# Seven half-size products for the first layers of the last two experts, in an attention and mixture-of-experts kernel

## The chip, the cores and the metric

One NeuronCore of a Trainium2 chip runs the whole program. The metric is the device time of one execution in microseconds. The kernel before took 952.56 us (median of 3 runs, 950.79 to 954.71).

## What is computed

Attention over 8 batches and 12 heads (448 tokens each, head size 64) gives x, 3584 tokens of 768 numbers. A router assigns every token to one of 8 experts, at most 448 tokens each, greedily from the highest logit down. Each expert is two matrix products with a ReLU between them:

```python
for e in range(E):
    mask = assigned == e
    h = np.maximum(x[mask] @ w1[e], 0.0)     # 448 x 768 @ 768 x 1024
    out[mask] = h @ w2[e]                     # 448 x 1024 @ 1024 x 768
```

## The kernel before, in words

The first half of the time is attention. Then the experts are processed one by one (here counted 0 to 7 in that order; the router picks the next one while earlier ones are computed, and that work is over within expert 5's first layer).

Everything is f32 in effect but runs as f16 pairs: a value is a high half h and a residue l, and a product is three matmuls, h by h, l by h and h by l. The **first layer** (`hidden`, L1640) makes the 1024 rows of the hidden layer in 8 blocks f of 128: 6 pieces of 128 of the inner size x 3 matmuls, each 128 x 128 weights against 448 tokens, summed in one PSUM bank (`ph`, 3 banks in turn). ScalarE applies the ReLU and writes the f16 half `hh` (L1659), VectorE the residue `hl` (L1661). The **second layer** (`result`, L1672) has the tokens in three chunks of 128 and one of 64. A chunk is two halves of 384 columns, each 24 matmuls into a `py` bank (3 in turn); ScalarE copies each half to `y` (3 buffers), and GpSimd scatters the rows of `y` to the output. The 64-token chunk uses half the array for each half of the columns.

Weights of the next expert come while this one is computed. `fetch` (L1564) has SP issue a DMA of 768 KB of f32 into one of 4 `stage` buffers; `split` (L1581) has ScalarE write the f16 half (L1590) and VectorE the residue in two instructions of 768 elements (L1594). There are 8 such pieces per expert, 4 of w1 and 4 of w2. `gather` (L1600) has GpSimd collect the expert's tokens into `rows`; DMA transposes (L1610) turn them into `xt`, 6 pieces of high halves and 6 of residues.

What order the instructions have is settled as the program is written out: every matmul advances a clock of estimated time (`tick`, L1710), pieces that are due by it are placed (`feed`, L1765, gives the due times), and what follows on VectorE is placed when ScalarE should be done (`later`, L1741). Each engine then runs its own queue strictly in that order. `run` (L1798) goes through the experts.

Of the kernel before, what the change touches and what calls it, by code (L numbers as in the profile page):

```python
# [37 lines left out]
class Plan:  # L38
# [51 lines left out]
class Attention:  # L90
# [1446 lines left out]
class Experts:  # L1537
# [19 lines left out]
    def load(self, k):  # L1557
        T = self.T
        e = self.router.e[k]
        T["reg", k] = self.nc.sync.value_load(e[:1, :1], min_val=0, max_val=7)  # L1560
        for n, a, f in (("w1h", 6, 1024), ("w1l", 6, 1024), ("w2h", 8, 768), ("w2l", 8, 768)):
            T[n, k] = self.w.tile([128, a, f], F16, name=n)

    def fetch(self, k, i, later=False):  # L1564

        T = self.T
        r = T["reg", k]
        s = self.w.tile([128, 1536], F32, name="stage", bufs=self.STAGES)
        if later:
            self.nc.gpsimd.memset(s[:, 0:1], 0.0)  # L1570
        if i < 4:
            src = self.w1[bass.ds(r, 1), :, 256 * i:256 * i + 256].rearrange("o (c p) f -> p (o c) f", p=128)
            v = s.rearrange("p (c f) -> p c f", c=6)
        else:
            j = 2 * (i - 4)
            src = self.w2[bass.ds(r, 1), 128 * j:128 * j + 256, :].rearrange("o (c p) f -> p (o c) f", p=128)
            v = s.rearrange("p (c f) -> p c f", c=2)
        self.nc.sync.dma_start(v, src)
        T["stage", k, i] = v

    def split(self, k, i):  # L1581
        T = self.T
        v = T.pop(("stage", k, i))
# [12 lines left out]
        if i + self.STAGES < 8:  # L1596
            self.later(0.0, lambda: self.fetch(k, i + self.STAGES), k, i)


    def gather(self, k):  # L1600
        nc, T = self.nc, self.T
        idx = self.router.idx[k]
        T["xt", k] = self.w.tile([128, 12, 448], F16, name="xt")
# [194 lines left out]
    def run(self):  # L1798
# [28 lines left out]
        for k in range(8):  # L1827
            self.now = k
            self.start()
            for f in range(8):  # L1830
# [3 lines left out]
                self.hidden(k, f)  # L1834
            self.need(k, 7)
# [50 lines left out]
```

## Time and profile before

| | |
|---|---|
| time of the runs, median | 952.56 us |
| profiled execution, its own time | 953.22 us |
| its span, first to last instruction | 951.0 us |
| mean granted TensorE clock | 0.988 |
| TensorE (matmuls) busy | 892.6 us, 94% |
| VectorE busy | 700.3 us, 74% |
| ScalarE busy | 512.1 us, 54% |
| GpSimd busy | 468.9 us, 49% |

The profile is that of one execution, taken by the hardware profiler, so durations in it are set against 953.22 us. A share of busy time is an average over very different stages; the rows further down are cut by stage.

### The profile page before, as it was taken

The page shows a single profiled execution, that of the slowest core. Times are in us where ns is not written, and L with a number is a line of the kernel's source. Part 1 is how long each engine was busy: PE and PEld are TensorE (multiplying, and loading weights), DVE is VectorE, ACT ScalarE, POOL GpSimd, SP SyncE. Part 2 cuts the span into 40 slices and gives each one's busy share as a digit, 9 for nine tenths or more (in the row PEclk, how much of TensorE's full clock was granted, in tenths as well). Part 3 has the DMA queues.
Part 4 walks back from the last instruction along what each step waited for, and adds up shares of the span by engine and source line. Part 5 has one row for each costly group of instructions (what it writes and reads, how often), then busy time and mean ns, then how long its engine had stood idle before and what let it go on. Part 6 is the DMA issues. An engine that isn't in the chain of part 4 may idle for free.

```text
span 951.0 us, 24928 instructions
## 1 busy us (share of the span) xinstructions
PE 892.6 (94%) x10335; PEld 573.7 (60%) x10336; DVE 700.3 (74%) x1562; ACT 512.1 (54%) x942; POOL 468.9 (49%) x463
## 2 busy tenths in 40 slices
PE   2799999999999999998699999999999999999996
PEld 1367767676777767757355556555565555655553
DVE  6999998899989988888787787786776758234110
ACT  5998978897888788653042424333332424243111
POOL 6889998999999899994000302121112020120001
PEclk9999999999999999999699999999999999999999
DMA  7558999997999987771272919494947649593001
GB/s 193 118 122 161 180 162 221 189 210 129 240 203 194 158 198 165 134 146 64 77 249 73 325 41 298 123 291 147 259 156 222 202 155 282 167 182 114 26 17 42
DMA packets 264230, 157.74 MB, mean 166 GB/s; under 512 B 189876, under 2 KB 251316, under 8 KB 263092
## 3 DMA queue, kind: packets, MB, share of 16 engines
q1 hardware_dynamic: 258674, 133.66, 60.5%
q0 software_dynamic: 4608, 22.02, 6.8%
q8 instruction: 81, 1.33, 0.6%
q10 hardware_dynamic: 834, 0.46, 0.2%
q14 instruction: 33, 0.27, 0.1%
HBM read 94.42 MB, written 22.02 MB: 122 GB/s over the span
## 4 chain that ended last, share of the span: by engine, by line
issue 36%; PE 35%; DVE 12%; DMA 6%; POOL 6%; ACT 3%; SPq 1%; POOLq 0%; DVEq 0%; ACTq 0%
PE po L571 8%; PE psc L528 6%; PE ph L1669 6%; DVE mx L506 4%; DMA kq<-s 3%; PE pm L497 3%; POOL rows L1607 3%; PE py L1686 2%; POOL out_dram L1702 2%; PE po L577 2%; PE psc L530 2%; PE po L581 2%; PE po L579 2%; DVE vs L468 2%; ACT e L536 1%
## 5 line engine op out<-in xcount | busy, mean ns | idle before, releaser
L1669 PE MATMUL ph<-xt,w1h 128*128 128x448 f16 (+2 forms) x804 | 209.7, 344 | 0.8 <-ACT xt L1626 0.5
L506 DVE TENSOR_REDUCE mx<-pm 128x2 f32<-128x896 f32 x162 | 175.8, 1085 | 25.3 <-PE pm L497 24.3
L552 POOL TENSOR_TENSOR pl<-e 128x896 f16<-128x896 f32 x105 | 182.3, 1748 | 10.6 <-ACT e L536 9.4
L1702 POOL DMA_INDIRECT out_dram<-y,idx x32 | 33.2, 1036 | 311.4 <-ACT y L1688 239.0
L536 ACT ACTIVATE e<-psc 128x896 f32<-128x896 f32 x168 | 148.8, 911 | 48.9 <-PE psc L530 47.5
L571 PE MATMUL po<-v,e 128*128 128x65 f32 (+1 forms) x960 | 156.9, 279 | 0.0
L571 PEld LDWEIGHTS po<-v,e 128*128 128x128 f32 (+1 forms) x960 | 120.0, 176 | 33.2 <-issue 31.7
L1669 PE MATMUL ph<-xt,w1l 128*128 128x448 f16 (+2 forms) x402 | 136.8, 344 | 0.0
L579 PE MATMUL po<-vs,e 128*128 128x64 f16 (+1 forms) x1056 | 131.2, 194 | 0.1
L577 PE MATMUL po<-vs,e 128*128 128x65 f16 (+1 forms) x1056 | 130.8, 195 | 0.3 <-DVE z L603 0.3
L581 PE MATMUL po<-vs,pl 128*128 128x65 f16 (+1 forms) x1056 | 129.8, 193 | 0.0
L528 PE MATMUL psc<-kq 64*128 64x448 f16 (+1 forms) x1152 | 124.2, 352 | 2.1 <-ACT e L536 1.2
L1686 PE MATMUL py<-w2h,hh 128*128 128x384 f16 x384 | 125.0, 326 | 0.0
L1686 PE MATMUL py<-w2h,hl 128*128 128x384 f16 x384 | 125.0, 326 | 0.0
L1686 PE MATMUL py<-w2l,hh 128*128 128x384 f16 x384 | 125.0, 326 | 0.0
L1659 ACT ACTIVATE hh<-ph 128x448 f16<-128x448 f32 x64 | 34.8, 543 | 145.6 <-PE ph L1669 131.3
L577 PEld LDWEIGHTS <-e 128*128 128x128 bf16 (+1 forms) x1056 | 109.8, 120 | 2.9 <-issue 1.9
L1669 PEld LDWEIGHTS <-w1h 128*128 128x128 f16 x804 | 74.0, 97 | 61.3 <-issue 1.5
L1686 PEld LDWEIGHTS <-hh 128*128 128x128 f16 x768 | 73.6, 97 | 45.8
L1688 ACT ACTIVATE y<-py 128x384 f32<-128x384 f32 x48 | 23.5, 491 | 132.4 <-PE py L1686 104.9
L1661 DVE SCALAR_TENSOR_TENSOR hl<-ph,hh 128x448 f16<-128x448 f32 x64 | 39.2, 618 | 71.2 <-ACT hh L1659 71.2
L581 PEld LDWEIGHTS <-pl 128*128 128x128 f16 (+1 forms) x1056 | 90.1, 101 | 0.2 <-issue 0.2
(274 smaller groups left out, 1811.3 us busy)
## 6 DMA issues: line engine op xcount, KB each, us to landing
stage<-in_moe_w_dram SPq DMA_DIRECT2D x64, 768.0 KB
vraw<-in_v_dram SPq DMA_DIRECT2D x24, 384.0 KB
xd<-xa SPq DMA_DIRECT2D x8, 1152.0 KB
qkraw<-in_q_dram SPq DMA_DIRECT2D x11, 768.0 KB
qkraw<-in_k_dram SPq DMA_DIRECT2D x11, 768.0 KB
vraw<-in_v_dram SPq DMA_DIRECT2D x48, 32.0 KB
xd<-xa SPq DMA_DIRECT2D x16, 96.0 KB
qkraw<-in_q_dram SPq DMA_DIRECT2D x22, 64.0 KB
```

Of the source, the lines that this page charges most:

```text
L506: self.nc.vector.tensor_reduce(m, p[r, :, :448], axis=AX.X, op=OP.max)
L528: mm(o, k[r, mine], q[r, all_], start=i == 0, stop=False)
L536: self.nc.scalar.activation(e, p[:, :, :448], AF.Exp, scale=scale)
L552: eng.tensor_tensor(l, self.T["e", d], self.T["ph", d], op=OP.subtract)
L571: nc.tensor.matmul(out, self.T["e", d][:, h, q0:q0 + m], self.v32[g % 2][:, 2 * h + a, wide.index(b % 4)], start=first, stop=last)
L577: nc.tensor.matmul(out, e[:, h, q0:q0 + m], vh, start=first, stop=False)
L579: nc.tensor.matmul(out[:, :64], e[:, h, q0:q0 + m], vl[:, :64], start=False, stop=False)
L581: nc.tensor.matmul(out, l[:, h, q0:q0 + m], vh, start=False, stop=last)
L1661: self.later(0.6, lambda: nc.vector.scalar_tensor_tensor(hl, whole, 0.0, hh, op0=OP.max, op1=OP.subtract), k, 3.5, f)
L1669: nc.tensor.matmul(p, a, b[:, o], start=st, stop=sp)
L1686: nc.tensor.matmul(p, a[:, f, s], b[:, f, o], start=st, stop=sp)
L1702: st = nc.gpsimd.indirect_dma_start(out=self.out, out_offset=bass.IndirectOffsetOnAxis(ap=self.router.idx[k][:n, c:c + 1], axis=0), in_=y[ ...
```

## The change

For experts 6 and 7 alone, the first layer is computed with w1 cut in halves both ways (A11, A12, A21, A22, each 384 of the inner size by 512 hidden rows) and the tokens likewise (two halves of the inner size, two of 224 tokens). Seven products of halves replace eight: A11 B11, A12 B21, and five products of sums. In each of 4 blocks i of 128 hidden rows (in both halves of the hidden layer) a product is 9 matmuls of 224 columns into a PSUM bank of its own (3 `ph`, 2 `py`, 2 `rp`), and VectorE and ScalarE combine the seven in f32 partial sums that lie in `orow`, the router's tile of one-hot rows ("or" in the rows), used here as two times 3 x 224 f32. Each of these has one buffer for all blocks.

- `fetch` brings quarters of w1. Of these A11, A12 and A22 are split as they are; then VectorE forms the four sums of quarters in place in `stage` (4 operations of 128 x 1536 f32, L1630), and the four sums are split too (`quarter`).
- `tokens` forms the four sums of the token halves on VectorE and splits them again.
- The splits of the sums and of w2 (for expert 6) are placed in the second layer of the expert before; for expert 7, w2 is split during its own first layer.
- Weights all come from two tiles, "wh" and "wl", with 4 buffers each; `xt` has 3 buffers, `y` has 2 where it had 3.

```diff
+    def quarter(self, k, i):
+        if i == 3:
+            a11, a12, a22, a21 = (T["stage", k, j] for j in range(4))
+            for o, x, y, op in ((a22, a21, a22, OP.add), (a21, a11, a21, OP.subtract), (a11, a22, a11, OP.subtract),
+                                (a12, a12, a11, OP.subtract)):
+                self.later(1.65, lambda o=o, x=x, y=y, op=op: V.tensor_tensor(o, x, y, op=op), k, i)
+            return
...
+        nc.scalar.activation(h, v, AF.Copy, scale=self.WS)
+        self.scalar(1.48)
+        for w in (slice(0, 768), slice(768, 1536)):
+            self.later(0.93, lambda w=w: V.scalar_tensor_tensor(l[:, w], v[:, w], self.WS, h[:, w], op0=OP.mult,
+                                                                op1=OP.subtract), k, i)
+        if more:
+            self.later(0.0, lambda: self.fetch(k, 4 + n), k, i)
+
+    def tokens(self, k):
...
+        V.tensor_tensor(f, x[:, :6], x[:, 6:], op=OP.add)
+        for o, a, b in ((b11, b12, b11), (b12, b22, b12), (b22, b22, b11), (b21, b21, b22)):
+            V.tensor_tensor(o, a, b, op=OP.subtract)
+        for j in (0, 3):
+            nc.scalar.activation(y[:, j:j + 3], f[:, j:j + 3], AF.Copy)
+            V.tensor_tensor(y[:, 6 + j:9 + j], f[:, j:j + 3], y[:, j:j + 3], op=OP.subtract)
...
+    SUMMED = 5.0, 2.4
+    SECOND = 18.0, 4.0
...
+    def seventh(self, k, i, n, j, h, p):
...
+        for c in range(3):
+            for a, b, st, sp in ((w, 0, c == 0, False), (w, 6, False, False), (v, 0, False, c == 2)):
+                nc.tensor.matmul(p, a[:, c], x[:, b + 3 * j + c], start=st, stop=sp)
+                self.tick(0.095)
+
+    def hidden7(self, k, i):
...
+        p1, p2, p6, p5, p7, p3, p4 = (
+            self.ps.tile([128, 512], F32, name=n, bufs=2 if n == "rp" else 3)[:, :224]
+            for n in ("ph", "py", "rp", "ph", "py", "rp", "ph"))
+        t = self.router.orow.rearrange("p g a t -> p (g a t)").bitcast(F32)
+        c1, c2 = (t[:, 672 * n:672 * n + 672].rearrange("p (n t) -> p n t", n=3) for n in range(2))
...
+        def relu(f, v):
+            v = v.rearrange("p n t -> p (n t)")
+            A.activation(hh[:, f], v, AF.Relu)
+            self.scalar(0.55)
+            V.scalar_tensor_tensor(hl[:, f], v, 0.0, hh[:, f], op0=OP.max, op1=OP.subtract)
+
+        self.seventh(k, i, 0, 0, 0, p1)
+        m = c2[:, 0]
+        A.activation(m, p1, AF.Copy)
+        self.scalar(0.35)
+        self.seventh(k, i, 1, 1, 0, p2)
+        self.seventh(k, i, 3, 1, 1, p6)
+        add(c1[:, 0], m, p2)
+        add(c1[:, 2], m, p6)
+        self.seventh(k, i, 5, 0, 0, p5)
+        add(c1[:, 1], c1[:, 2], p5)
+        self.seventh(k, i, 6, 0, 1, p7)
+        add(c2[:, 2], c1[:, 2], p7)
+        add(c2[:, 1], c2[:, 2], p5)
+        self.seventh(k, i, 4, 1, 1, p3)
+        add(c1[:, 1], c1[:, 1], p3)
+        relu(i, c1[:, 0:2])
+        self.seventh(k, i, 2, 1, 0, p4)
+        add(c2[:, 0], c2[:, 2], p4)
+        relu(i + 4, c2[:, 0:2])
...
-        y = self.w.tile([128, 768], F32, name="y", bufs=3)
+        y = self.w.tile([128, 768], F32, name="y", bufs=2)
```

**The order on VectorE, late in expert 5's first layer.** "or" are the router's one-hot rows, "hl" a block's residue, "wl"/"w1l" a split of weights, "stage" the sums of weights. Before:

```order
L1491 TENSOR_TENSOR or<-ar,rows_9263 128x1536
L1594 SCALAR_TENSOR_TENSOR w1l<-stage,w1h 128x3x256 x2
L1661 SCALAR_TENSOR_TENSOR hl<-ph,hh 128x448 x2
L1594 SCALAR_TENSOR_TENSOR w1l<-stage,w1h 128x3x256
L1502 COPY idlo<-rp 128x4
L1504 SCALAR_TENSOR_TENSOR idx<-rp,idlo 128x4
```

With the change:

```order
L1491 TENSOR_TENSOR or<-ar,rows_9263 128x1536
L1797 SCALAR_TENSOR_TENSOR hl<-ph,hh 128x448
L1641 SCALAR_TENSOR_TENSOR wl<-stage,wh 128x768 x2
L1630 TENSOR_TENSOR stage<-stage 128x1536 x4
L1797 SCALAR_TENSOR_TENSOR hl<-ph,hh 128x448 x2
L1502 COPY idlo<-rp 128x4
L1504 SCALAR_TENSOR_TENSOR idx<-rp,idlo 128x4
```

The first "hl" is that of block 3 in both. The residue of block 4, next to it before, stands behind two splits and the four sums of expert 6's weights now. Ahead of this piece four splits have been placed since the residue of block 0, where there were two.

**The order on VectorE in expert 6's first layer,** from the last operations of block 1 to the third addition after the sums in block 2. Before (any part of that stage):

```order
L1594 SCALAR_TENSOR_TENSOR w1l<-stage,w1h 128x3x256 x2
L1661 SCALAR_TENSOR_TENSOR hl<-ph,hh 128x448
L1594 SCALAR_TENSOR_TENSOR w1l<-stage,w1h 128x3x256 x2
L1661 SCALAR_TENSOR_TENSOR hl<-ph,hh 128x448
L1594 SCALAR_TENSOR_TENSOR w1l<-stage,w1h 128x3x256 x2
```

With the change:

```order
L1713 SCALAR_TENSOR_TENSOR hl<-or,hh 128x448
L1641 SCALAR_TENSOR_TENSOR wl<-stage,wh 128x768 x2
L1707 TENSOR_TENSOR or<-or,ph 128x224
L1713 SCALAR_TENSOR_TENSOR hl<-or,hh 128x448
L1641 SCALAR_TENSOR_TENSOR wl<-stage,wh 128x768 x2
L1707 TENSOR_TENSOR or<-or,py 128x224
L1707 TENSOR_TENSOR or<-or,rp 128x224
L1630 TENSOR_TENSOR stage<-stage 128x1536 x4
L1707 TENSOR_TENSOR or<-or,ph 128x224
L1707 TENSOR_TENSOR or<-or,py 128x224
L1707 TENSOR_TENSOR or<-or,ph 128x224
```

Splits of expert 7's quarters and the four sums for expert 7 stand between the additions that read and so free the banks.

**The order on ScalarE in the same stage,** blocks 0 to 2 ("or" is the copy of p1, "hh" the ReLU, "wh" a split). Before:

```order
L1659 ACTIVATE hh<-ph 128x448 x2
L1590 ACTIVATE w1h<-stage 128x6x256
L1659 ACTIVATE hh<-ph 128x448
L1590 ACTIVATE w1h<-stage 128x6x256
L1659 ACTIVATE hh<-ph 128x448
```

With the change:

```order
L1717 ACTIVATE or<-ph 128x224
L1711 ACTIVATE hh<-or 128x448 x2
L1717 ACTIVATE or<-ph 128x224
L1638 ACTIVATE wh<-stage 128x1536 x2
L1711 ACTIVATE hh<-or 128x448 x2
L1638 ACTIVATE wh<-stage 128x1536
L1717 ACTIVATE or<-ph 128x224
L1711 ACTIVATE hh<-or 128x448 x2
```

Two splits stand between the copy and the ReLU of block 1, and a third ahead of the copy of block 2.

## Rows read from the trace of the kernel before

**Rows 1.** Busy time by stage: layers 1 and 2 of experts 5, 6, 7 (us).

```profile
core 0: us, PE busy (x) PEld busy (x) DVE busy (x) ACT busy (x) POOL busy (x), PEclk, DMA share, GB/s
776.20:805.50 29.30, 29.30 (x208) 16.15 (x207) 24.95 (x67) 11.64 (x14) 5.43 (x6) 1.00 1.05 285
805.50:833.00 27.50, 27.50 (x193) 16.62 (x191) 6.11 (x7) 7.60 (x10) 3.23 (x6) 1.00 0.55 188
833.00:860.30 27.30, 27.30 (x147) 14.13 (x146) 12.95 (x17) 11.64 (x14) 4.79 (x6) 1.00 0.94 204
...
887.80:915.00 27.20, 27.20 (x146) 14.09 (x145) 4.37 (x7) 4.77 (x9) 0.99 (x2) 1.00 0.04 8
```

**Rows 2.** Timeline of TensorE, matmuls of 128 and 448 columns: start, length.

```profile
482.98 0.28 PE L1669 MATMUL ph<-xt,w1h 128*128 128x128 f16 x2
...
483.14 0.28 PE L1669 MATMUL ph<-xt,w1h 128*128 128x128 f16 x2
...
888.75 0.35 PE L1669 MATMUL ph<-xt,w1l 128*128 128x448 f16 x1
...
889.32 0.35 PE L1669 MATMUL ph<-xt,w1l 128*128 128x448 f16 x1
```

**Rows 3.** Groups by shape since 440 us: count, busy us, mean ns, idle before.

```profile
L1669 PEld LDWEIGHTS <-w1h 128*128 128x128 f16 x804 | 74.0, 97 | 61.3 <-issue 1.5
...
L1594 DVE SCALAR_TENSOR_TENSOR w1l<-stage,w1h 128x768 f16<-128x768 f32 x64 | 59.3, 950 | 3.4 <-ACT w1h L1590 3.4
L1590 ACT ACTIVATE w1h<-stage 128x1536 f16<-128x1536 f32 x32 | 47.3, 1477 | 23.5 <-DVE placed L1453 21.0 <-DMA stage<-in_moe_w_dram 2.5
...
L1491 DVE TENSOR_TENSOR or<-ar,rows 128x1536 bf16<-128x1536 bf16 x8 | 7.6, 950 | 0.0
...
L1165 DVE SCALAR_TENSOR_TENSOR logits<-esel,logits 128x224 f32<-128x224 f32 x7 | 2.7, 383 | 0.0
...
L1245 DVE TENSOR_TENSOR or<-key,unit 128x640 f32<-128x640 f32 x2 | 1.6, 812 | 0.0
...
L1245 DVE TENSOR_TENSOR or<-key,unit 128x256 f32<-128x256 f32 x2 | 0.8, 407 | 0.0
```

**Rows 4.** Timeline of VectorE, expert 5's first layer.

```profile
792.77 2.08 DVE L1491 TENSOR_TENSOR or<-ar,rows 128x2048 bf16<-128x2048 bf16 x2
794.77 1.82 DVE L1594 SCALAR_TENSOR_TENSOR w1l<-stage,w1h 128x768 f16<-128x768 f32 x2
```

**Rows 5.** Timeline of ScalarE: ReLU of expert 5's block 6, two results of expert 7.

```profile
802.30 0.54 ACT L1659 ACTIVATE hh<-ph 128x448 f16<-128x448 f32 x1 [2.42 <-PE ph L1669]
...
919.19 0.49 ACT L1688 ACTIVATE y<-py 128x384 f32<-128x384 f32 x1 [3.41 <-PE py L1686]
...
926.99 0.49 ACT L1688 ACTIVATE y<-py 128x384 f32<-128x384 f32 x1 [3.46 <-PE py L1686]
```

**Rows 6.** Timeline of all engines, end of expert 7's first layer.

```profile
914.85 0.35 PE L1669 MATMUL ph<-xt,w1l 128*128 128x448 f16 x1
...
915.24 0.54 ACT L1659 ACTIVATE hh<-ph 128x448 f16<-128x448 f32 x1 [2.86 <-PE ph L1669]
...
915.82 0.62 DVE L1661 SCALAR_TENSOR_TENSOR hl<-ph,hh 128x448 f16<-128x448 f32 x1 [2.78 <-ACT hh L1659]
```

**Rows 7.** DMA issues of the page, weights.

```profile
stage<-in_moe_w_dram SPq DMA_DIRECT2D x64, 768.0 KB
```

**Rows 8.** Timeline of GpSimd, first scatter of expert 7.

```profile
923.81 0.97 POOL L1702 DMA_INDIRECT out_dram<-y,idx  x1 [33.61 <-ACT y L1688]
```

**Rows 9.** Busy time by microsecond near the end, columns as in rows 1.

```profile
927.00:928.00 1.00, 1.00 (x8) 0.59 (x7) 0.00 (x0) 0.48 (x1) 0.00 (x0) 1.00 0.00 0
...
942.00:943.00 1.00, 0.63 (x8) 0.20 (x4) 0.00 (x0) 0.28 (x1) 0.00 (x0) 1.00 0.05 18
...
948.00:949.00 1.00, 0.00 (x0) 0.00 (x0) 0.00 (x0) 0.00 (x0) 0.00 (x0) 0.50 0.00 0
```

More of the change, by code (lines that the diff above doesn't have):

```diff
@@ L1570, in fetch @@
             self.nc.gpsimd.memset(s[:, 0:1], 0.0)
-        if i < 4:
+        if k in self.SEVEN and i < 4:
+            a, b = self.QUARTERS[i]
+            src = self.w1[bass.ds(r, 1), 384 * b:384 * b + 384, 512 * a:512 * a + 512]
+            src = src.rearrange("o (c p) f -> p (o c) f", p=128)
+            v = s.rearrange("p (c f) -> p c f", c=3)
+        elif i < 4:
             src = self.w1[bass.ds(r, 1), :, 256 * i:256 * i + 256].rearrange("o (c p) f -> p (o c) f", p=128)
@@ L1582, in split @@
         T = self.T
+        if k in self.SEVEN and i < 4:
+            return self.quarter(k, i)
         v = T.pop(("stage", k, i))
@@ L1597, in split @@
             self.later(0.0, lambda: self.fetch(k, i + self.STAGES), k, i)
+    SEVEN = 6, 7
+    QUARTERS = (0, 0), (0, 1), (1, 1), (1, 0)
+    SUMS = {3.2: 0, 3.4: 1, 3.6: 2, 3.8: 3}
+    def quarter(self, k, i):
+        nc, T = self.nc, self.T
+        V = nc.vector
+        if i == 3:
[4 more added lines that the diff above has]
+            return
+        if i == 3.05:
+            return self.tokens(k)
+        more = i > 3
+        n = self.SUMS[i] if more else i
+        v = T["stage", k, n].rearrange("p c f -> p (c f)")
+        h, l = (T[w, k + 0.5 * more].rearrange("p a f -> p (a f)")[:, 1536 * n:1536 * n + 1536] for w in ("w1h", "w1l"))
+        nc.scalar.activation(h, v, AF.Copy, scale=self.WS)
[5 more added lines that the diff above has]
+            self.later(0.0, lambda: self.fetch(k, 4 + n), k, i)
@@ new lines, in tokens @@
+    def tokens(self, k):
+        nc, T = self.nc, self.T
+        V = nc.vector
+        x, y = T["xt", k], T["xt", k + 0.5]
+        f = self.w.tile([128, 4, 1536], F16, name="rows", bufs=1).rearrange("p c d -> p (c d)").bitcast(F32)
+        f = f[:, :2688].rearrange("p (n c) -> p n c", n=6)
+        b11, b12, b21, b22 = (f[:, 3 * j:3 * j + 3, 224 * h:224 * h + 224] for j in (0, 1) for h in (0, 1))
+        V.tensor_tensor(f, x[:, :6], x[:, 6:], op=OP.add)
[4 more added lines that the diff above has]
+            V.tensor_tensor(y[:, 6 + j:9 + j], f[:, j:j + 3], y[:, j:j + 3], op=OP.subtract)
@@ new lines, in sums, with second @@
+    def sums(self, k):
+        T = self.T
+        for low in [low for low in self.lows if low[3][1:2] == (3.5,)]:
+            self.low(low)
+        self.need(k, 3)
+        self.halves("w1", k + 0.5)
+        T["xt", k + 0.5] = self.w.tile([128, 12, 448], F16, name="xt", bufs=3)
+        for n, i in enumerate((3.05, *self.SUMS)):
+            self.fill(self.SUMMED[0] * (n > 0) + self.SUMMED[1] * n, k, i)
+        if k < 7:
+            self.second(k)
+    def second(self, k):
+        for n in range(4):
+            self.fill(self.SECOND[k - 6] + 2.4 * n, k, 4 + n)
@@ new lines @@
+    SUMMED = 5.0, 2.4
+    SECOND = 18.0, 4.0
+    def seventh(self, k, i, n, j, h, p):
+        nc, T = self.nc, self.T
+        more = n > 2
+        w, v = (T[a, k + 0.5 * more].rearrange("p a f -> p (a f)")[:, 1536 * (n - 3 * more):1536 * (n - 3 * more) + 1536]
+                .rearrange("p (c f) -> p c f", c=3)[:, :, 128 * i:128 * i + 128] for a in ("w1h", "w1l"))
+        sums = n in (2, 3, 5, 6)
+        x = T["xt", k + 0.5 * sums][:, :, 224 * h:224 * h + 224]
+        for c in range(3):
+            for a, b, st, sp in ((w, 0, c == 0, False), (w, 6, False, False), (v, 0, False, c == 2)):
+                nc.tensor.matmul(p, a[:, c], x[:, b + 3 * j + c], start=st, stop=sp)
+                self.tick(0.095)
@@ L1602, in gather @@
         idx = self.router.idx[k]
-        T["xt", k] = self.w.tile([128, 12, 448], F16, name="xt")
+        T["xt", k] = self.w.tile([128, 12, 448], F16, name="xt", bufs=3)
         g = T["rows", k] = self.w.tile([128, 4, 1536], F16, name="rows", bufs=1)
@@ L1768, in feed @@
             self.fetch(k, i)
-        for i in range(8):
-            self.fill(self.PIECE[0] + self.PIECE[1] * i, k, i)
+        more = k in self.SEVEN
+        for i in range(4 if more else 8):
+            self.fill(self.PIECE[0] + (2.6 if more else self.PIECE[1]) * i, k, i)
     def step(self, k, i):
@@ L1829, in run @@
             self.start()
-            for f in range(8):
+            if k == 7:
+                self.halves("w2", k)
+                self.second(k)
+            if k in self.SEVEN:
+                self.need(k, 3.9)
+                for i in range(4):
+                    self.hidden7(k, i)
+            for f in range(0 if k in self.SEVEN else 8):
                 self.need(k, f // 2)
@@ L1834, in run @@
                 self.hidden(k, f)
+            if k + 1 in self.SEVEN:
+                self.sums(k + 1)
             self.need(k, 7)
```

17 lines of the change are left out of this document (15 added, 2 removed).

## Prediction

> **What bounds the kernel now.** I cut the last three experts at the hand-over from layer to layer and asked for the busy time of each engine by stage [rows 1]. The reader is to see two things. TensorE is busy for the whole of every stage: 27.3 and 27.2 us in the first layers of experts 6 and 7 (the last two; I count 0 to 7 in the order of processing), at clock 1.00. So every us of products saved there is a us of span, and every us for which TensorE has to wait is one lost. And VectorE has 24.95 us of work in the 29.3 us of expert 5's first layer, 12.95 in expert 6's, 4.37 in expert 7's. The change puts its new work into just these three stages, so I priced VectorE's instructions [rows 3], then walked its queue, which is in order.
>
> **The products, -6.3 us.** A 448-column matmul takes 0.57 / 3 = 0.19 us from start to start, one of 128 columns 0.16 / 3 = 0.053 us, each with a weight load of its own [rows 2]. On the line between them 224 columns take 0.094 us; 0.097 us, the time of one load [rows 3], is the upper bound if loads of neighbouring matmuls could not overlap. I take 0.0955, near half of 0.19. Per expert 4 blocks x 7 products x 9 matmuls = 252 x 0.0955 = 24.1 us replace 27.25 us (the mean of the two stages): 3.15 us each, 6.3 in all. One product lasts 0.86 us, a block of seven 6.03 us. The second layers keep their matmuls.
>
> For the stationary loads the Trainium skill ("TensorE: Matmul & The Clock Gate", section "LDWEIGHTS (loading the stationary operand)") gives columns / 1.2 in ns, 107 ns for 128 columns. By that rule, as an estimate, 252 x 0.107 = 27.0 us would be left, 0.3 us per expert would be saved instead of 3.15, and the sum below would be 5.7 us higher. The trace speaks against it: 128-column matmuls, each with a load, follow each other every 0.053 us [rows 2].
>
> **Prices on VectorE and ScalarE.** A split of 768 takes 0.95 us, and 0.87 from start to start, because neighbours overlap by 0.08 (1.82 us for two: [rows 3, 4]). For the f32 sums in SBUF the nearest rows are f32 tensor-tensor operations of 256 and 640 elements, 407 and 812 ns [rows 3]: 1.05 ns an element, so 1536 take 1.75 us, 1.67 from start to start, four 6.7 us. The lower bound is the 16-bit operation on 1536 elements, 950 ns [rows 3], 0.87 from start to start. An addition of 224: the scalar-tensor-tensor of 224 takes 383 ns [rows 3]; with overlap 0.30, where the next one needs its result 0.41, on average 0.36. No row shows one with a PSUM operand of this size; 0.30 and 0.42 are my ends. A ScalarE split of 1536 is 1.48 [rows 3]; ReLU of 448 columns 0.54, a result of 384 columns 0.49, so on that line a copy of 224 is 0.36 [rows 5]. The residue of 448 is 0.62, by start 0.54 [rows 6]. Hand-overs: ScalarE begins 0.20 us behind the end of the last matmul's 0.19 us slot (914.85 + 0.19 to 915.24), VectorE 0.04 behind ScalarE [rows 6].
>
> **Place 1, expert 5's first layer: +4.0 us.** The four sums of weights for expert 6 stand on VectorE ahead of the residue of block 4 (the order before and after stands above), and the three "ph" banks let block 7 begin only when that residue has been read. Before, the one-hot rows are done at 794.77 [rows 4]. After, two more splits stand ahead of them: 794.77 + 1.74 = 796.5; residue 3 to 797.05; two splits to 798.8; four sums to 805.5; residue 4 to 806.0, hand-over 806.1. TensorE would begin block 7 at 802.1 (ReLU of block 6 starts at 802.30, less 0.20 [rows 5]). It waits 4.0 us. The data are there: the four fetches of 768 KB [rows 7] are issued at the start of this stage, and 3.1 MB at 285 GB/s [rows 1] take 11 us.
>
> **Expert 5's second layer: 0.** It gets the token sums (estimated at 8.9 us from the rates above), eight splits of sums and eight of second-layer weights (13.9 us), 23 us where 6.11 are busy now, in 27.5 us [rows 1]. ScalarE evicts the first result some 6 us late, behind the tokens; the three "py" banks, 3.9 us of matmuls each, cover that. The second-layer fetches now stand on SP behind the sums' splits; they have some 10 us to land. With two "y" buffers instead of three a result waits for the scatter before last, which left a chunk earlier, 7.8 us (919.19 to 926.99 [rows 5]); a scatter issued at 923.81 [rows 8] has moved its bytes by 927 [rows 9]. If a transfer is late by 3 us, it costs what ScalarE then holds up, at most 1 us.
>
> **Place 2, expert 6's first layer: +8.6, and +2.0 behind it.** A block without foreign work costs the VectorE-ScalarE chain: copy 0.40, six additions 2.2, ReLU and hand-overs 0.65, residue 0.54, one addition, ReLU, residue again 1.5: 5.3 us, under TensorE's 6.03. The partial sums have one buffer, so the copy of the next block waits for the last residue of this one. In blocks 1 and 2 six splits (5.2 us), three ScalarE splits and four sums (6.7) are inserted, 12 us of VectorE in 12 us of TensorE. From the stage's start T: last residue of block 0 at T+8.5; copy 8.9; two additions 9.7; VectorE then waits for ScalarE's split, 10.4; two splits 12.15; four additions, ReLU, residue 14.8; two splits 16.5; addition, ReLU, residue 18.1; ScalarE's third split ends at 18.95 and the copy for block 2 at 19.3; two splits 20.7; two additions 21.4; four sums 28.1; three additions 29.2. Only then is the bank free that product p5 of block 3 needs; at its own pace TensorE would be there at 3 x 6.03 + 3 x 0.86 = T+20.7. It starts at 29.3: 8.6 us late, 1.3 and 0.4 of it spent at two products before, so the longest single hole is about 7. The layer then ends at T+32.75, and the last block's chain (copy 32.8, six additions 35.0, ReLU, residue 36.1) is still behind: the second layer, which comes to block 3 after 9 matmuls of 0.1625 us (7.8 / 48), waits 1.7 for it and 0.3 for a late "py" bank.
>
> **Place 3, expert 7: +2.0, and +1.7 behind it.** No sums, but eight splits of second-layer weights (7.0 us on VectorE, 4 x 1.48 on ScalarE) in blocks 0 and 1. The same walk has the copy of block 2 at T+19.4 against TensorE's need at 18.1, smaller waits of 0.2 to 0.3 at three further products, 2.0 in all, and again 1.7 for block 3's residue.
>
> **Sum.** -6.3 + 4.0 + 8.6 + 2.0 + 2.0 + 1.7 = +12.0 us, on the profiled execution's 953.22: 965.2. That execution is 0.66 above the median of 952.56, so 964.6; I say 965. Bounds: some 42 additions lie on the walks of the two experts, so 0.30 or 0.42 for one moves the sum by -2.5 or +2.5; sums at 0.87 by -6.4.
>
> **Rivals.**
> *VectorE keeps pace (ends on the other side).* Banks and the idle half of VectorE in expert 6's stage [rows 1] swallow everything: 946.3, or 948 with the waits behind the layers. For it: each of the seven products has a bank, so TensorE can run most of a block ahead, and 5.3 is under 6.03. Against it: backlog 8.6, of which sums are 6.7, so even free sums leave 1.9. It decides at the bank of p5: VectorE must be through block 2's third addition by T+20.7, with sums and additions both some two thirds of my prices. 6%. With that only nearly so, the gain is paid back: no change, 953. 10%.
> *Fast sums.* At 0.87 each, place 1 is 0.8 and place 2 5.4: 6.4 less, 958. The 16-bit row is for it, both f32 rows against. 14%.
> *Loads bind, or the clock falls.* If the loads, 0.097 us each [rows 3], overlap so badly that a matmul comes every 27.25 / 252 = 0.108 us, the saving is gone; but TensorE then waits less at places 2 and 3, which hides most of it, and 1 to 3 us remain. The Trainium skill's rule on loads, above, is this case. A hole of 7 us may also cost the clock: TensorE ends within the us from 942, at clock 1.00, and in the us from 948 the granted clock is 0.50 [rows 9]. The 3.4 us of block 3 at 1.2 GHz would take 3.4 more, half of it covered by the wait behind it. 967 to 971. 8%.
> That the change doesn't do what it says: the order has nine matmuls of 224 columns for each of seven products; excluded.
>
> **How the numbers follow.** Forecast 62%. A measurement tells 0.5%, 4.8 us, from no change. Slower by more: 62 + 14 + 8 = 84%; within: 10%; faster: 6%. The range leaves out those last two, 16%: from fast sums with quick additions, 958 - 2.5, to 971: 956 to 971.
>
> **What would show it.** A wait of TensorE for VectorE of about 4 us at expert 5's block 7; one of some 7 us at the fourth product of expert 6's last block; waits of 1 to 2 us at the second layers' tenth matmul; sums of 1.75 us; first layers of about 33 and 26 us against 27.25, 224-column matmuls 0.0955 us apart. The forecast is wrong if the sums take 0.95 us, if the additions take under 0.3, or if VectorE's residues are not held behind the sums.

## The result, and the profile after

The changed kernel takes 968.87 us (median, 966.57 to 969.66) against 953.63 us of the kernel before in the same series (950.79 to 955.77): ratio 1.0146, 95% interval 1.0108 to 1.0183. It is slower by 15.2 us; 965 with a range of 956 to 971 had been forecast. The profiled execution took 969.66 us, with a span of 967.9. From its page, the span, the engines' busy time, and the granted clock in 40 slices (tenths):

```profile
span 967.9 us, 25494 instructions
...
PE 897.1 (93%) x10551; PEld 597.2 (62%) x10552; DVE 761.0 (79%) x1652; ACT 528.0 (55%) x960; POOL 469.7 (49%) x463
...
PEclk9999999999999999997699999999999999988998
```

VectorE has 61 us more work than before, TensorE 4.5 more busy us although it has fewer columns to stream: slices near the end stand at 8, where the clock fell. Where that is, the stages tell.

Next the windows of the kernel after, cut where TensorE begins a layer of experts 5, 6 and 7. The columns are the window, its length, the busy time of each engine with its count of instructions, the granted clock, the DMA share and the rate. They answer to [rows 1].

```profile
core 0: us, PE busy (x) PEld busy (x) DVE busy (x) ACT busy (x) POOL busy (x), PEclk, DMA share, GB/s
778.33:813.36 35.03, 30.88 (x209) 16.50 (x208) 28.23 (x67) 8.89 (x12) 5.42 (x6) 0.95 0.60 174
813.36:840.87 27.51, 27.51 (x193) 16.63 (x191) 22.45 (x22) 16.88 (x17) 4.16 (x6) 1.00 0.52 180
840.87:876.68 35.81, 27.54 (x255) 25.92 (x253) 27.01 (x45) 10.58 (x17) 5.27 (x6) 0.86 0.60 154
876.68:904.20 27.52, 27.52 (x195) 16.64 (x193) 17.87 (x18) 11.23 (x14) 4.00 (x6) 1.00 0.46 158
904.20:930.07 25.87, 24.71 (x254) 24.15 (x253) 17.75 (x35) 11.04 (x16) 0.99 (x2) 1.00 0.04 10
930.07:959.51 29.44, 27.93 (x194) 16.47 (x192) 3.61 (x9) 4.17 (x9) 3.17 (x6) 1.00 0.10 41
```

Before, TensorE was busy for the whole of every stage. Now two stages have grown by 6 to 9 us, in both of them TensorE is idle for a part, and in both the mean clock is under 1.00 (0.95 and 0.86). The last stage, the second layer of expert 7, has 1.5 us of idle time. Expert 7's first layer is the only one that gained.

This table has the time between the first matmuls of successive layers (the last column runs to the end of the last matmul), in us, read in the same way from TensorE's timeline of every profiled execution. The experiments below are judged by it, because it leaves out what the stages ahead vary by from one execution to the next: the start of expert 5 lies at 776.2 before and 778.3 after, and anywhere from 776.5 to 783.0 in the runs below. "And chain cut" is "both undone" with the three later edits described below (the copy's place, the new order, the late residues).

| kernel | 5 first | 5 second | 6 first | 6 second | 7 first | 7 second | sum |
|---|---|---|---|---|---|---|---|
| before | 29.28 | 27.52 | 27.25 | 27.51 | 27.25 | 27.59 | 166.40 |
| after | 35.03 | 27.51 | 35.81 | 27.52 | 25.87 | 29.44 | 181.18 |
| place 1 undone | 29.28 | 27.52 | 34.36 | 27.92 | 25.88 | 29.45 | 174.41 |
| place 2 undone | 36.47 | 27.51 | 26.06 | 29.37 | 25.89 | 29.45 | 174.75 |
| sums on GpSimd | 29.28 | 32.51 | 26.11 | 34.29 | 25.88 | 29.44 | 177.51 |
| holes filled | 33.59 | 27.51 | 33.35 | 29.37 | 25.88 | 29.44 | 179.14 |
| both undone | 29.28 | 27.51 | 26.06 | 29.37 | 25.87 | 29.44 | 167.53 |
| and chain cut | 29.28 | 27.52 | 24.33 | 27.52 | 24.39 | 27.59 | 160.63 |

The loss of 14.8 us in the stages is nearly all of the measured 15.2. Then the waits of TensorE in the kernel after, from expert 5 on. The columns are tile and line that waited, who released it, the sum in us, how many, and the longest.

```profile
PE ph L1689 <- DVE or L1707: 7.2, 2, 7.0
PE ph L1805 <- DVE hl L1797: 4.2, 1, 4.2
PE ph L1689 <- ACT or L1717: 1.9, 2, 1.0
PE py L1822 <- ACT hh L1711: 1.3, 1, 1.3
PE rp L1689 <- DVE or L1707: 0.3, 1, 0.3
PE py L1822 <- DVE hl L1713: 0.2, 1, 0.2
```

The 4.2 us stand at expert 5's block 7, the 7.0 at product p5 of expert 6's last block. VectorE's timeline, which answers to [rows 4], shows what it does meanwhile (start, duration, engine, line, operation, tiles, count):

```profile
798.95 1.81 DVE L1641 SCALAR_TENSOR_TENSOR wl<-stage,wh 128x768 f16<-128x768 f32 x2
800.79 7.14 DVE L1630 TENSOR_TENSOR stage<-stage 128x1536 f32<-128x1536 f32 x4
807.85 1.15 DVE L1797 SCALAR_TENSOR_TENSOR hl<-ph,hh 128x448 f16<-128x448 f32 x2
...
861.84 0.38 DVE L1707 TENSOR_TENSOR or<-or,rp 128x224 f32<-128x224 f32 x1
862.14 7.13 DVE L1630 TENSOR_TENSOR stage<-stage 128x1536 f32<-128x1536 f32 x4
869.18 0.38 DVE L1707 TENSOR_TENSOR or<-or,ph 128x224 f32<-128x224 f32 x1
```

Both times four sums of weights stand between VectorE and the instruction that frees TensorE's bank: the residue at 807.85, the additions from 869.18. TensorE's own timeline has the other side:

```profile
808.52 0.90 PE L1805 MATMUL ph<-xt,wh 128*128 128x448 f16 x2 [4.15 <-DVE hl L1797]
...
870.34 0.53 PE L1689 MATMUL ph<-xt,wh 128*128 128x224 f16 x2 [7.04 <-DVE or L1707]
```

The same windows by the microsecond (window, length, TensorE busy with its matmuls, granted clock, DMA share, rate) show the part that the forecast left to a rival, and answer to [rows 9]:

```profile
807.00:808.00 1.00, 0.00 (x0) 1.00 0.00 0
808.00:809.00 1.00, 0.48 (x2) 0.53 0.00 0
...
811.00:812.00 1.00, 1.00 (x5) 0.77 0.00 0
...
865.00:866.00 1.00, 0.00 (x0) 1.00 0.00 0
866.00:867.00 1.00, 0.00 (x0) 0.54 0.00 0
...
875.00:876.00 1.00, 1.00 (x7) 0.50 0.00 0
876.00:877.00 1.00, 1.00 (x9) 0.84 0.00 0
```

In both holes the clock falls to 0.50, 1.2 GHz. At place 1 it is back in the us from 811; at place 2 the last four products of the layer, 36 matmuls from 870.34 to 876.68, run at half speed: 6.34 us, where 36 x 0.0955 is 3.44.

### The profile page after: what moved, and what is told of

Its sections match the earlier page's. It is cut to its first block, busy times and chain, and to the rows that moved or that the text cites. A ratio compares the mean times of both kernels' runs of the same rounds, so it can differ in the third digit from the quotient of the medians.

```text
span 967.9 us, 25494 instructions
## 1 busy us (share of the span) xinstructions
PE 897.1 (93%) x10551; PEld 597.2 (62%) x10552; DVE 761.0 (79%) x1652; ACT 528.0 (55%) x960; POOL 469.7 (49%) x463
## 4 chain that ended last, share of the span: by engine, by line
issue 37%; PE 36%; DVE 11%; POOL 5%; DMA 5%; ACT 3%; SPq 2%; POOLq 0%; DVEq 0%; ACTq 0%
PE po L571 8%; PE psc L528 7%; PE ph L1805 5%; DVE mx L506 4%; PE pm L497 3%; POOL rows L1743 3%; POOL out_dram L1838 3%; PE py L1822 2%; PE psc L530 2%; PE po L577 2%; PE po L579 2%; PE po L581 2%; DVE vs L468 2%; DMA kq<-s 2%; ACT e L536 1%
## 5 line engine op out<-in xcount | busy, mean ns | idle before, releaser
L1838 POOL DMA_INDIRECT out_dram<-y,idx x32 | 35.4, 1105 | 324.8 <-ACT y L1824 253.5
L1805 PE MATMUL ph<-xt,wh 128*128 128x448 f16 (+2 forms) x612 | 158.8, 343 | 4.9 <-DVE hl L1797 4.2
L1822 PE MATMUL py<-wh,hh 128*128 128x384 f16 x384 | 125.0, 326 | 1.3 <-ACT hh L1711 1.3
L1822 PE MATMUL py<-wh,hl 128*128 128x384 f16 x384 | 125.0, 326 | 0.2 <-DVE hl L1713 0.2
L1822 PE MATMUL py<-wl,hh 128*128 128x384 f16 x384 | 125.0, 326 | 0.0
L577 PEld LDWEIGHTS <-e 128*128 128x128 bf16 (+1 forms) x1056 | 109.8, 120 | 2.9 <-issue 1.9
L1607 DVE SCALAR_TENSOR_TENSOR wl<-stage,wh 128x768 f16<-128x768 f32 x112 | 104.7, 951 | 4.5 <-ACT wh L1603 4.4
L1805 PE MATMUL ph<-xt,wl 128*128 128x448 f16 (+2 forms) x306 | 103.4, 343 | 0.0
L1603 ACT ACTIVATE wh<-stage 128x1536 f16<-128x1536 f32 x56 | 82.7, 1476 | 26.8 <-DVE placed L1453 21.1
L1795 ACT ACTIVATE hh<-ph 128x448 f16<-128x448 f32 x48 | 26.1, 543 | 116.7 <-PE ph L1805 113.6
L579 PEld LDWEIGHTS <-e 128*128 128x128 bf16 (+1 forms) x1056 | 89.3, 102 | 0.0
```

What stands on the lines that cost most here:

```text
L577: nc.tensor.matmul(out, e[:, h, q0:q0 + m], vh, start=first, stop=False)
L579: nc.tensor.matmul(out[:, :64], e[:, h, q0:q0 + m], vl[:, :64], start=False, stop=False)
L1805: nc.tensor.matmul(p, a, b[:, o], start=st, stop=sp)
L1822: nc.tensor.matmul(p, a[:, f, s], b[:, f, o], start=st, stop=sp)
```

## Experiments

**The memory alone.** The kernel before, with the shared weight tiles, three buffers of `xt` and two of `y`, and full products.

```diff
+            t = self.w.tile([128, 6144], F16, name="w" + n[2], bufs=4)
+            T[n, k] = t.rearrange("p (a f) -> p a f", f=f)
...
-        y = self.w.tile([128, 768], F32, name="y", bufs=3)
+        y = self.w.tile([128, 768], F32, name="y", bufs=2)
```

> The kernel before with the change's memory alone: wh and wl from shared tiles of 4 buffers, three buffers of xt, two of y instead of three; eight full products as before. Theory (VectorE's queue holds the banks, and TensorE waits at three places; the memory costs nothing): the time of before, 953.6 us, within 2. Rival (memory): if two y buffers or the shared weight tiles hold up evictions, splits or fetches, some of the change's 15 us appears here already: 957 or more, with TensorE waiting for ScalarE in the second layers of the last experts.

Measured: 954.26 us against 954.44, ratio 0.9996 (0.9976 to 1.0015). The six stages sum up to the 166.40 us of the kernel before. No cost of the memory can be seen; that rival is out.

**Place 1 undone.** The same four sums for expert 6, each as a due piece of its own, so that expert 5's residues come in between.

```diff
-            for o, x, y, op in ((a22, a21, a22, OP.add), (a21, a11, a21, OP.subtract), (a11, a22, a11, OP.subtract),
...
+            for o, x, y, op in every if k == 7 else every[round(100 * (i - 3)):][:1]:
...
+        for j in range(1, 4) if k == 6 else ():
+            self.fill(self.PIECE[0] + 2.6 * 3 + 3.4 * j, k, 3 + 0.01 * j)
```

> The changed kernel, with the four sums of weights for expert 6 put into VectorE's queue one by one, between the residues of expert 5's last blocks and not ahead of them. Same work, another order. Theory: place 1 alone goes away. Block 7 of expert 5 no longer waits (4.15 us in the changed kernel), and the clock does not fall there (some 1.5 us): 968.9 - 5.7 = 963.2, 961.5 to 965. Place 2 keeps its 7-us wait and its clock of 0.50. Rival (the work itself, wherever it stands): 967 to 970, as VectorE does as much as in the changed kernel. Rival (clock falls by the new products and not by a wait): the dip at 808 us goes, but not the time, within 2 us of 968.9.

Measured: 964.99 us, ratio 1.0108 (1.0082 to 1.0133). Expert 5's first layer takes 29.28 us, to the hundredth what it took before; 7.0 us of wait at place 2 remain. Ordering VectorE's queue differently, with no work removed, gives 5.75 us back in that stage. Place 2 changes too, although nothing was done there: its layer takes 34.36 us instead of 35.81, because behind the same 7.04-us wait (matmuls again from 864.75) the clock is back sooner, and the second layer behind it takes 0.4 us more:

```profile
867.00:868.00 1.00, 1.00 (x8) 0.62 0.00 0
```

In all the stages give 6.8 us back. The times of the runs give only 3.6 to 3.9 (the intervals leave room for more); the stages are the sharper measure.

**Place 2 undone.** Expert 7's sums stand in expert 6's second layer, behind the token sums; the splits of the sums, which follow them, are due 8.6 us later in that layer too.

```diff
-        self.need(k, 3)
+        self.need(k, 3 if k == 6 else 2)
...
+        if k == 7:
+            self.fill(0.5, k, 3.1)
```

> The changed kernel, with the four sums of weights for expert 7 moved from expert 6's first layer into its second layer, behind the token sums. Same work. Theory: place 2 loses its long wait (7.04 us at product p5 of block 3 becomes 0 to 1) and with it the stretch at clock 0.50 (2.9 us in the last four products); the first layer of expert 6 goes from 35.8 to about 26 us; behind it the wait of 1.5 us that expert 7 shows comes up for expert 6 too: 968.9 - 9.9 + 1.5 = 960.5, 958.5 to 962.5. VectorE has then 23 us of work in the second layer of 27.5; if that is too much, TensorE waits at the first products of expert 7 instead, for up to 3 us, and the time is 963. Rival (clock falls because 224-column products are too light a load, not because of the hole): clock near 0.50 late in expert 6's first layer stays, and only the 7 us go: 962 to 964.

Measured: 961.99 us, ratio 1.0070 (1.0048 to 1.0092). Expert 6's first layer takes 26.06 us (about 26 expected), clock 1.00 there, and the wait behind it appears: the second layer takes 29.37. So the slow clock belongs to the hole and not to products of 224 columns. At place 1 nothing was changed and the wait is the same 4.17 us, but the clock stays low for longer and the stage takes 36.47 us, 1.44 more than in the kernel after:

```profile
807.00:808.00 1.00, 0.00 (x0) 0.54 0.00 0
808.00:809.00 1.00, 0.92 (x3) 0.50 0.00 0
...
813.00:814.00 1.00, 1.00 (x5) 0.55 0.00 0
```

**The sums on GpSimd.** It does little in these stages.

```diff
-                self.later(1.65, lambda o=o, x=x, y=y, op=op: V.tensor_tensor(o, x, y, op=op), k, i)
+                self.later(0.0, lambda o=o, x=x, y=y, op=op: nc.gpsimd.tensor_tensor(o, x, y, op=op), k, i)
```

> The changed kernel, with the eight sums of weights (both experts) on GpSimd instead of VectorE, in place. GpSimd's f32 operations of 896 in the attention take 1.8 to 2.1 us, so one of 1536 3.1 to 3.6 and four 12 to 14 us. Theory: places 1 and 2 both lose what the sums put there: 968.9 - 5.7 - 8.4 = 954.8, 953 to 958, which is the kernel before's time within the error; what is left are the waits of expert 7's first layer and behind the layers. Splits of sums wait for GpSimd at most 1 us. Rival (the two engines slow each other): VectorE's operations beside GpSimd's sums grow by a third or more, and the holes come back in part: 958 to 964. Rival (sums are not the cause): 967 to 970.

Measured: 965.27 us, ratio 1.0109 (1.0084 to 1.0133). Both holes are gone from the first layers (29.28 and 26.11 us), as the theory says, but the time is back in the second layers (32.51 and 34.29). This is the rival, and at more than the 964 it was given. GpSimd's timeline (three of its eight sums) and VectorE's of this run:

```profile
811.98 6.02 POOL L1630 TENSOR_TENSOR stage<-stage 128x1536 f32<-128x1536 f32 x1
...
865.12 3.70 POOL L1630 TENSOR_TENSOR stage<-stage 128x1536 f32<-128x1536 f32 x1
...
872.67 3.87 POOL L1630 TENSOR_TENSOR stage<-stage 128x1536 f32<-128x1536 f32 x1
```

```profile
809.50 5.21 DVE L1653 TENSOR_TENSOR rows<-xt 128x2688 f32<-128x2688 f16 x1
814.75 6.64 DVE L1655 TENSOR_TENSOR rows<-rows 128x672 f32<-128x672 f32 x4
...
863.19 0.38 DVE L1707 TENSOR_TENSOR or<-or,rp 128x224 f32<-128x224 f32 x1
...
866.47 2.84 DVE L1713 SCALAR_TENSOR_TENSOR hl<-or,hh 128x448 f16<-128x448 f32 x1 [0.64 <-ACT hh L1711]
...
874.20 2.83 DVE L1713 SCALAR_TENSOR_TENSOR hl<-or,hh 128x448 f16<-128x448 f32 x1 [0.64 <-ACT hh L1711]
```

Beside GpSimd's sums the token sums take 5.21 us (2.95 after expert 6's, when GpSimd is idle) and 6.64 (3.54), and some residues from the partial sums 2.84 instead of 0.62. Additions that read a PSUM bank keep their 0.38. The rows fit engines that take turns. The two slow residues end at 869.31 and 877.03, each 0.49 us behind the end of a GpSimd sum (868.82 and 876.54). The sum at 811.98, with the token sums beside it, takes 6.02 us, where the three ahead of it took 3.43. The residue at 874.20 is the one for which TensorE's second layer waits at 877.08. The one at 866.47 holds up ScalarE's copy for block 3, then VectorE's additions and the ReLU for which TensorE waits 4.25 us. In expert 5's second layer ScalarE, behind the late token sums, evicts too late:

```profile
823.18 0.32 PE L1822 MATMUL py<-wh,hh 128*128 128x384 f16 x1 [3.16 <-ACT y L1824]
...
872.65 0.50 PE L1822 MATMUL py<-wh,hh 128*128 128x384 f16 x1 [4.25 <-ACT hh L1711]
877.08 0.34 PE L1822 MATMUL py<-wh,hl 128*128 128x384 f16 x1 [0.65 <-DVE hl L1713]
```

**The holes filled.** Matmuls that nobody reads, a little shorter than each hole.

```diff
+            if (k, f) == (5, 7):
+                self.warm(17)
...
+        if (k, i) == (6, 3):
+            self.warm(30)
```

> The changed kernel, with matmuls that nobody reads put into TensorE's two long waits: 17 of 512 columns ahead of block 7 of expert 5, 30 ahead of product p5 of block 3 of expert 6, a little less than fills the waits. Theory (the clock falls because TensorE stands still, and costs 1.5 us at place 1 and 2.9 at place 2): clock 1.00 at both places, the last four products of expert 6's first layer 3.4 us instead of 6.3; the waits themselves stay, as the banks come free no sooner, and behind place 2 some 1.9 us of wait come up that the slow products had covered. First layer of expert 5 33.5 us (35.0 in the changed kernel), of expert 6 32.9 (35.8), second layer of expert 6 29.4 (27.5): 2.5 us less, 966.4. Rival (the clock falls for another reason, light products or VectorE's load): clock and time as in the changed kernel, 968.9 within 1.

Measured: 966.05 us, ratio 1.0125 (1.0099 to 1.0152). The times of the runs alone can't tell this from the kernel after; the stages can. The clock is 1.00 in all six, and the three of the forecast are 33.59, 33.35 and 29.37 us (33.5, 32.9 and 29.4 expected). So the clock cost 1.4 us at place 1 and 2.5 at place 2, and 1.9 of that had covered the wait behind place 2:

```profile
867.00:868.00 1.00, 0.44 (x4) 1.00 0.00 0
868.00:869.00 1.00, 1.00 (x13) 1.00 0.00 0
```

**Both undone.** The two edits together.

```diff
-        self.need(k, 3)
+        self.need(k, 3.04 if k == 6 else 2)
```

> The sums of both experts out of TensorE's way: those of expert 6 one by one between the residues of expert 5, those of expert 7 in expert 6's second layer. Theory (places 1 and 2 are independent): the stages add up, 29.3 + 27.5 + 26.1 + 29.4 + 25.9 + 29.4 = 167.6 us against 166.4 in the kernel before: the same time as before, ratio 1.001 (0.998 to 1.004). What is left of the cost is then about 1.9 us of waits in each first layer of seven products and 1.9 behind each, which give back the 6.3 us of saved products. Rival (a third cost that has been hidden): 958 or more.

Measured: 954.39 us against 953.97, ratio 1.0014 (0.9991 to 1.0036); stages 167.53 us. With both places gone the saved products (6.3 us) just about pay for what is left: 1.7 to 1.9 us of waits in each of the two first layers and 1.9 behind each. In the stages 1.1 us of loss remain, which the times of the runs can't tell from no change. Where they stand, the places gave back 5.75 us (35.03 to 29.28) and 7.9 (35.81 and 27.52 to 26.06 and 29.37) when undone one at a time, together the 13.65 that both undone give back. So but for what the clock did at the untouched place the two are independent.

**A place for the copy; a new order in the second layer.** Two small edits on top, in turn: the first product's copy lies in 224 unused columns of `orow`, and the first token chunk takes hidden blocks 3 and 7 last, for both halves.

```diff
-        m = c2[:, 0]
+        m = t[:, 1344:1568]
...
+            for half, fs in (((0, (0, 1, 2, 4, 5, 6)), (1, (0, 1, 2, 4, 5, 6)), (0, (3, 7)), (1, (3, 7))) if late else
```

> As the run with both sums out of the way, and the copy of the first product gets a place of its own in the tile of partial sums, so that ScalarE can free the bank without waiting for the residue of the block before. Theory (one buffer of partial sums makes the 0.9 and 1.0 us waits for ScalarE's copy at the first products of blocks 2 and 3): these waits go in both experts, 1.9 us each, unless VectorE's backlog is as late at the next bank: 0.5 to 3.8 us less than that run, most likely 2.5; ratio to before 0.998. Rival (VectorE's backlog alone decides): the waits move by one product to VectorE's additions, no gain, ratio 1.001.

> As the run before it, and in the second layers of experts 6 and 7 the first token chunk takes the hidden blocks 3 and 7, whose residues come last, behind the six others of both halves (two banks open at once). Theory (the 1.9 us behind each first layer are the chain of block 3's additions, ReLU and residue): TensorE has 36 matmuls, 5.8 us, before it needs them instead of 9, and both waits go: second layers of 27.5 us instead of 29.4, 3.8 us less than the run before it: ratio to before 0.994, 948 to 950. Rival (the late py bank, or ScalarE behind its queue, holds the second layer up as well): 1 to 2 us less only.

Measured: 954.39 us, ratio 1.0003 (0.9987 to 1.0019), and 953.36 us, ratio 0.9989 (0.9971 to 1.0007). Neither can be told from no change. The first forecast, most likely 2.5 us less, did not come out, and the second, 0.994, failed. In the stages the two give 166.45 and 165.85 us, against 167.53 with both places undone. With the copy free, the wait in expert 7 moved on by two products, to VectorE's addition (0.97 became 0.86), much as the rival had it. In expert 6 it stayed (0.96): there a ScalarE split, 850.86 to 852.33, stands just ahead of the copy. With the new order, expert 7's second layer fell to 27.58 us as expected, but expert 6's only to 28.60 (28.80 in the run before it) and its first layer rose to 27.00. The waits of this run:

```profile
PE ph L1692 <- ACT or L1720: 1.2, 1, 1.2
PE rp L1692 <- DVE or L1710: 1.2, 2, 0.9
PE py L1828 <- ACT y L1832: 0.9, 1, 0.9
PE ph L1692 <- DVE or L1710: 0.8, 3, 0.4
```

**VectorE's chain cut; the splits spaced.** In the chain of a block VectorE twice stood idle 0.64 us for ScalarE's ReLU. The residue of the first half now stands behind the next addition, that of the second behind the next block's first two. The second run spreads the foreign splits as well, one piece every 5 us.

```diff
-            V.scalar_tensor_tensor(hl[:, f], v, 0.0, hh[:, f], op0=OP.max, op1=OP.subtract)
+            return lambda: V.scalar_tensor_tensor(hl[:, f], v, 0.0, hh[:, f], op0=OP.max, op1=OP.subtract)
...
         add(c1[:, 2], m, p6)
+        if i:
+            self.pending()
...
+        low()
+        self.pending = relu(i + 4, c2[:, 0:2])
...
-            self.fill(self.SECOND[k - 6] + 2.4 * n, k, 4 + n)
+            self.fill(18.0 + 2.4 * n if k == 6 else 2.0 + 5.0 * n, k, 4 + n)
```

> As the run with the second layer's new order, and VectorE no longer stands waiting for ScalarE's ReLU: the residue of the first half is issued behind the next addition, that of the second half behind the first two additions of the next block (0.64 us of idle time, twice a block, goes). Theory (what is left in the first layers, 26 to 27 us against 252 x 0.0957 = 24.1, is VectorE's chain per block of 5.3 us plus the splits): the chain falls to about 4.2 us a block, and the waits at the products of blocks 2 and 3 shrink by 1 to 2 us in each expert: 950.5 to 952, ratio 0.997. Rival (ScalarE's weight splits, 1.47 us each, standing ahead of the copy that frees the bank): the wait for ScalarE's copy, 1.2 us in expert 6, stays, and the gain is under 1 us.

> As the run before it, and the weight splits spread: the three quarters of expert 7 in expert 6's first layer and the four pieces of its second-layer weights in its own come every 5 us, one a block, and the splits of expert 7's sums in expert 6's second layer come later, so that ScalarE does not wait for VectorE's sums with a result to evict behind it. Theory (both engines' foreign work then fits into each block): first layers of 24.3 to 25 us, second layers of 27.6; stages 29.3 + 27.5 + 24.6 + 27.6 + 24.6 + 27.6 = 161.2 us against 166.4 before: 948.5, 947 to 950, ratio 0.994 to 0.995. Rival (a first layer's 24.1 us is too short for VectorE's and ScalarE's work in any order): first layers stay near 26, ratio 0.998 or more.

Measured: 947.70 us against 954.65, ratio 0.9929 (0.9911 to 0.9947), better than the 0.997 expected; spaced, 948.01 us, ratio 0.9927 (0.9907 to 0.9947), the same; its first layers are the shortest of all, 24.17 and 24.16 us. The view of waits lists none for TensorE from expert 5 on, in either run. These windows, of the first of the two runs, answer to those of the kernel after:

```profile
838.21:862.54 24.33, 24.32 (x254) 24.16 (x253) 18.79 (x40) 10.69 (x16) 5.78 (x8) 1.00 0.91 241
862.54:890.06 27.52, 27.52 (x194) 16.62 (x193) 25.29 (x25) 12.01 (x14) 5.55 (x6) 1.00 0.25 85
890.06:914.45 24.39, 24.32 (x254) 24.16 (x253) 18.82 (x39) 10.79 (x16) 0.99 (x2) 1.00 0.24 92
914.45:942.04 27.59, 27.59 (x194) 16.62 (x192) 2.16 (x6) 3.98 (x8) 3.17 (x6) 1.00 0.11 43
```

So seven products can gain: 2.9 us per expert in the first layers, 5.8 us in the stages, 7 in the runs. VectorE does as much as in the kernel after (115.4 us in these six stages against 116.9); only where it does it has changed. This version beats both kernels. Whether the late residues would do it without the copy's place and the new order, no run shows.

**The chain cut alone.** The three later edits (the copy's place, the new order, the late residues), with the sums where the change has them.

```diff
-        m = c2[:, 0]
+        m = t[:, 1344:1568]
...
-        relu(i, c1[:, 0:2])
+        low = relu(i, c1[:, 0:2])
```

> The changed kernel with its sums where they are, and only the three later edits: a place of its own for the copy, the second layer's new order, VectorE's residues behind the next additions. Theory (the sums make places 1 and 2, the chain the rest): place 1 stays as it was, first layer of expert 5 35 us; the hole at product p5 of block 3 shrinks from 7 to some 5 us, as the chain of blocks 0 to 2 gives VectorE back about 1.1 us each, and the clock still falls in it, first layer of expert 6 30 to 32; both second layers 27.5, first layer of expert 7 24.4: 171 to 173 us of stages against 166.4 before, 958 to 961. Rival (the chain was the real cause of the backlog, and the sums fit once it is shorter): expert 6's hole under 2 us, 955 or less, all of the loss beyond place 1 gone.

Measured: 963.13 us, ratio 1.0092 (1.0066 to 1.0117). Stages 35.28, 27.51, 33.92, 27.52, 24.39 and 27.58 us, in sum 176.20; 958 to 961 had been expected, by a hole of 5 us.

```profile
867.20 0.53 PE L1689 MATMUL ph<-xt,wh 128*128 128x224 f16 x2 [7.06 <-DVE or L1707]
```

The hole is 7.06 us, about as long as the four sums (7.13), although the chain is shorter. VectorE comes to the sums 19.7 us into the layer, not 21.3, but TensorE comes to p5 earlier too, as its waits at the copy and at p6 (0.90 and 0.33) are gone. So the place of the sums makes the hole, with the chain cut as without; the three later edits together take away the small waits around it.

## Why the prediction was right

**The mechanism.** The forecast was 965.2 on the profiled execution, +12.0; in the stages +14.8 came out, by the mechanism that was forecast, at the places forecast. Undoing either place by order alone removed its wait and left the wait of the other as it was (7.0 and 4.17 us); what the clock took at the other place changed by 1.4 us, down in one run and up in the other. Counted where they stand, the two added up (5.75 and 7.9 to 13.65). The walk through VectorE's queue at place 2 held step by step: the four sums began 21.3 us into the layer (21.4 forecast), ended at 28.4 (28.1), and product p5 began at 29.5 (29.3).

**Products, -6.3.** Right, as [rows 2, 3] had it: in the spaced run 252 matmuls follow each other every 0.0959 us. An expert's first layer without waits takes 24.2 to 24.4 us (24.1 forecast). The rule on weight loads ("TensorE: Matmul & The Clock Gate", section "LDWEIGHTS (loading the stationary operand)" of the Trainium skill), by which 252 of them would have taken 27.0 us, is not what these 224-column products show: 24.2 us per expert in the spaced run, loads overlapped.

**Place 1, +4.0: 5.75.** The wait was 4.15 us. The rest is the clock, which the forecast here left out.

**Expert 5's second layer, 0.** Right: 27.51 us against 27.52, with 22.45 us of work on VectorE where 23 had been estimated.

**Place 2, +8.6 and +2.0 behind it: 11.7 and 0.** The layer was forecast to end 32.75 us after its start and took 35.81, 11.7 more than the 24.1 of its products. Its waits, 0.90, 0.33 and 7.04, make 8.3, near the forecast. The difference is the clock: 2.9 us by the last four products, 2.5 by the run with filled holes. That same slowness let VectorE catch up, so that of the 2.0 behind the layer nothing was left; with the clock kept up, 1.86 of it came out (29.37 against 27.51). The rival had it so (3.4 us more, half covered by the wait behind), with 8%, and the measured 968.9 lies in that rival's 967 to 971; its other half, loads that bind, did not occur. As a mechanism the clock belonged in the forecast. That 965 is close all the same is in part because the slow stretch hid 1.9 us of its own cost.

**Place 3, +2.0 and +1.7: 1.8 and 1.85.** Right (25.87 and 29.44 us against 24.1 and 27.59).

**The prices.** The four sums took 7.13 us, not 6.7: 1.79 from start to start, with none of the overlap of neighbours that the forecast had supposed. The runs don't show why: the second sum reads nothing that the first has written, and it too starts 1.79 behind it. Additions took 0.38, 0.30 to 0.41 from start to start, as forecast.

**The sum, by the mis-sized term.** The step that was too small is the one that ended in 965: no cost for the clock in the two holes, +1.4 and +2.5, against 1.9 that the slow products then hid behind the layer. That nets 2.0 of the 2.8 us missed in the stages: with the holes filled the stages are 12.7 us over the kernel before (179.14 against 166.40), where 12.0 had been forecast, and with the clock's fall 14.8. The sums, 0.4 us longer at each of two places, are large enough for the remaining 0.7; no run shows that share by itself.

**The rivals.** "VectorE keeps pace" was wrong about this kernel and right about what is possible: TensorE needs VectorE to be through the third addition that follows the sums in block 2 (the block's fifth; "block 2's third" in the forecast) in time, and in the version with the sums moved and the chain cut it is, at 947.7. Fast sums did not occur (1.76 us each against the 0.87 supposed).

## What to carry to other kernels

Before an engine with an in-order queue gets long foreign work, look for the instruction behind it that frees a bank, and put the long work behind that one: the same eight sums cost 13.7 us in the change's order (181.18 against 167.53) and no wait in another. Price a hole in TensorE's stream as its length plus the slow stretch behind it. Here the saving of products paid only once the chain that combines them left room for the foreign work beside it: a chain of about 5.3 us a block (the forecast's figure), under the products' 6.03, was not short enough. A shorter chain and another order of the foreign work changed a loss of 1.5% into a gain of 0.7%, with the same instructions on VectorE.

## What the runs showed of the hardware

**The clock.** A wait of 1.35 us left it at 1.00. Waits of 3.2, 4.2 and 7.0 us were followed by 1.2 GHz. Behind the 3.16 us of the run with sums on GpSimd it fell only after the matmuls had begun again at 823.18:

```profile
824.00:825.00 1.00, 1.00 (x5) 0.59 0.08 16
```

The same 4.2-us wait of expert 5 cost 1.4 us more in the run with place 2 undone than in the kernel after (36.47 against 35.03 us), and the same 7.0-us wait of expert 6 left its layer 1.5 us shorter with place 1 undone (34.36 against 35.81), so the price of a hole is not fixed by its length. With the holes filled the clock did not fall in these stages.

**VectorE beside GpSimd.** f32 sums of 1536 on GpSimd took 3.43 us in four of eight cases, 3.7 to 3.9 in three and 6.02 beside the token sums. What VectorE did from SBUF alone meanwhile grew up to 4.6 times (0.62 to 2.84), while additions with an operand in PSUM did not change. The Trainium skill ("SBUF — State Buffer", section "Who interferes with whom") says that a VectorE instruction with two inputs in SBUF contends with a GpSimd instruction that reads SBUF, and that the ports they share are locked by one engine at a time; these rows agree, as the slow residues end 0.49 us behind a GpSimd sum. An idle GpSimd was no free place for work beside VectorE's critical instructions.
